# Next chunk's transposes moved from TensorE to the DMA queue, with q/k and output products re-placed, in a fused attention and feed-forward kernel

## The chip, the cores and the metric

The kernel runs on one core of one Trainium2 chip. The metric is the device time of one execution in microseconds. Thirteen runs of the kernel before have a median of 184.62 us, from 183.6 to 185.64.

## The reference

`x` has 2048 positions of 448 features. It is layer-normalised once, and two branches read the result. `_A_ref` is a dilated local attention with 16 heads of 28 features: each position looks at itself and at seven earlier ones, two apart. `_B_ref` is a feed-forward block with 1792 hidden features. The branches are multiplied and added to the input.

```python
xn = _layernorm(x, axis=-1)
# _A_ref(xn): H = 16; Dh = 28; W, dil = 8, 2
qkv = (xn @ wqkv)...                       # 448 -> 3*448
idx = pos[:, None] - off[None, :]          # off = 0, 2, ..., 14
logits = einsum("bhsd,bhswd->bhsw", q, k[idx]) * Dh ** -0.5   # masked where idx < 0
o = einsum("bhsw,bhswd->bhsd", softmax(logits), v[idx])
s = o.reshape(B, S, D) @ wo
# _B_ref(xn):
h = gelu(xn @ w1 + b1)                     # 448 -> 1792, tanh form
g = silu(h @ w2 + b2)                      # 1792 -> 448
out = x + s * g
```

## The kernel before

**Tiles and chunks.** The even positions are put first and the odd ones after them, so that the dilation becomes a plain window of eight. The 2048 rows are 16 tiles of 128 and four chunks of four tiles. The feature dimension of 448 is four blocks of up to 128 (`KT`); the last is repeated to fill 128 rows, so that two products with 64 rows can run beside each other (`ffn1_rest`, L233).

**Layer norm.** For a tile, `ln_stats` (VectorE) and `ln_rstd` (ScalarE) give mean and scale, and `ln_apply` (L164) writes the normalised rows to `xnb`, of which there are four. `ln_tr` (L172) turns them with four TensorE transposes into a PSUM tile `pT`, and `ln_put` (L176) copies that to `xnT`, features by positions. All products read `xnT`.

**Attention.** `q_job` and `k_job` make four heads of q or k for one chunk: four matmuls of 512 columns (L188) and a copy from PSUM (L191). `v_job` makes v for one unit (L203, L208). A unit is 121 positions; there are 17. `qk_unit` computes the scores of all heads into two `psA` tiles (L312), `Exp` on ScalarE (L317) and a mask on VectorE (L319). `av_unit` multiplies with v into `psO` (L328) and spreads the denominators (L332); the `norm` that it returns is two ScalarE operations (L335, L336) and one on VectorE (L337), which writes `oT`.

**Feed-forward.** `feed_forward_1(c, ...)` is the first product of chunk c, in seven steps k of two hidden tiles each; `gelu` (L239) reads each from PSUM and writes `hT`. `ffn2_job(t)` is the second product of tile t (L257, 14 matmuls) with the bias added on VectorE (L264); `silu_job` is a tanh on ScalarE (L268) and an operation on VectorE (L269). `wo_job(t)` is the output product (L288), the multiplication with the feed-forward branch and the addition of x (L294, L297), and the store (L298).

**PSUM.** `psA` has two tiles of two banks, shared by scores and feed-forward steps. `psB` has four tiles of one bank for everything else; steps k = 0, 3 and 6 of the first product take two of them each.

**Order.** The instructions of TensorE, ScalarE, VectorE and GpSimd run in the order in which the program is written. The loads and stores are on the SP queue; the 16 loads of `wo` (L134) are the last of the loads in it. Chunk 0 is prepared with TensorE transposes and ScalarE copies. Then for c = 0, 1, 2: `feed_forward_1(c)`, with the four tiles' transposes of chunk c+1 in steps 0 and 2 (two tiles after each), silu of chunk c-1 in the same steps, and four q/k jobs of chunk c+1 in step 4; then the phase change with two more q/k jobs; then five attention units, beside which stand the second products of chunk c, the last q/k jobs and the v jobs of chunk c+1. `feed_forward_1(3)`, two units and the remaining output products end the program. The Gelu and the Exp operations need different ScalarE tables, so each `feed_forward_1` has a table load at either end (L351, L377). In chunks 2 and 3 the list `wos` gives output products to the steps from k = 2 on.

At the start `busy(8)` gives TensorE matmuls on zeros. A memset of eight pad columns of `wraw` (L125) stands in VectorE's order after the loads were issued.

Of the kernel before, what the change touches and what calls it, by code (L numbers as in the profile page):

```python
# [8 lines left out]
F32 = mybir.dt.float32  # L9
# [13 lines left out]
QB = 121  # L23
QW = 122
NB = 17
LEAD = 8
LQ = LEAD + S + 24
SCALE = 1.0 / math.sqrt(DH)
EPS = 1e-5
NG = 12  # L30
# [3 lines left out]
def kernel(  # L34
# [19 lines left out]
    def dram_rows(par, t0, n):  # L54
        cls, r = divmod(t0 * P, S // 2)
        return par[cls, r:r + n * P, :].rearrange("(t p) d -> p t d", p=P)
# [36 lines left out]
        return x_sb[t // 4][:, t % 4, :]  # L93


    nc.vector.memset(wz[:].bitcast(U32), 0)
    nc.vector.memset(eps_t[:], EPS)
    for t in range(4):
        (nc.sync, nc.scalar)[t % 2].dma_start(x_sb[0][:, t, :], dram_rows(x_par, t, 1)[:, 0, :])
    for dst, c0, c1 in ((wv, 2 * D, 3 * D), (wraw, 0, 2 * D)):  # L100
        nc.sync.dma_start(dst[:, 0:3, 0:c1 - c0], A_wqkv[0:384, c0:c1].rearrange("(k p) f -> p k f", p=P))
        nc.sync.dma_start(dst[:64, 3, 0:c1 - c0], A_wqkv[384:448, c0:c1])
    nc.sync.dma_start(b1t[:], B_b1.rearrange("(m f) -> f m", f=P))
    for c0, c1 in ((0, F // 2), (F // 2, F)):
        nc.sync.dma_start(w1[:, 0:3, c0:c1], B_w1[0:384, c0:c1].rearrange("(k p) f -> p k f", p=P))
        for r in (0, 64):
            nc.sync.dma_start(w1[r:r + 64, 3, c0:c1], B_w1[384:448, c0:c1])
        if c0 == 0:
            nc.sync.dma_start(x_sb[1][:, :, :], dram_rows(x_par, 4, 4))
    nc.sync.dma_start(w2[:, :, :], B_w2.rearrange("(m p) c -> p m c", p=P))  # L110
    nc.sync.dma_start(b2bc[:], B_b2.rearrange("(o d) -> o d", o=1).to_broadcast((P, D)))
    nc.sync.dma_start(x_sb[2][:, :, :], dram_rows(x_par, 8, 4))
# [9 lines left out]
    nc.gpsimd.memset(vw[:, :, :, 0:1], 1.0)  # L122
    nc.gpsimd.memset(vw[:, :, :, DH + 1:32], 0.0)
    nc.vector.memset(wv[64:128, 3, :].bitcast(U32), 0)
    nc.vector.memset(wraw[:, :, 2 * D:2 * D + 8].bitcast(U32), 0)  # L125
    nc.vector.memset(wraw[64:128, 3, 0:2 * D].bitcast(U32), 0)
    nc.vector.memset(wo[:, :, :].bitcast(U32), 0)
    for tl in (qT, kT):
# [25 lines left out]
    def ln_stats(t):  # L154
        st = work.tile([P, 6], F32, name="st", tag="st", bufs=4)
        nc.vector.bn_stats(out=st[:], in_=xt(t))
        nc.vector.bn_aggr(out=mv[:, t, :], in_=st[:])
# [11 lines left out]
    def ln_tr(t):  # L169
        pT = psB.tile([P, KT, P], BF16, name="pT", tag="B")  # L170
        for kt in range(KT):
            nc.tensor.transpose(pT[:, kt, :], xnb[t % 4][:, kt * P:(kt + 1) * P], ident[:])  # L172
        return pT

    def ln_put(t, pT, copy):
        copy(xnT[:, :, LEAD + t * P:LEAD + (t + 1) * P], pT[:, :, :])  # L176


    def qk_weights(which, kt):
# [13 lines left out]
    def q_job(c, g):  # L193
        qk_job(c, g, 0, nc.vector.tensor_copy)

    def k_job(c, g, copy=None):
        qk_job(c, g, 1, copy or nc.scalar.copy)
# [14 lines left out]


    def ffn1_tiles(k):
        if k % 3 == 0:
            return [psB.tile([P, CH], F32, name="ps_h", tag="B") for _ in range(2)]
        ps = psA.tile([P, 2, CH], F32, name="ps_h", tag="A")
        return [ps[:, i, :] for i in range(2)]
# [47 lines left out]
    def silu_job(t):  # L266
        th = work.tile([P, D], BF16, name="th", tag="th", bufs=2)
        nc.scalar.activation(th[:], y_sb[:, t % 4, 0:D], ACT.Tanh, scale=0.5)  # L268
        nc.vector.scalar_tensor_tensor(out=g_sb[t % NG][:], in0=th[:], scalar=1.0, in1=y_sb[:, t % 4, 0:D],  # L269
                                       op0=ALU.add, op1=ALU.mult)  # L270
# [72 lines left out]
    def busy(n):  # L343

        ps = psB.tile([P, CH], F32, name="ps_w", tag="B")
        for _ in range(n):
            nc.tensor.matmul(ps[:, :], wz[:, 0:P], wz[:, :], start=True, stop=True)

    def feed_forward_1(c, ps, wos):

        nc.scalar.preload_act_table_set(SET_GELU)  # L351
        nx = 4 * (c + 1)
        gelu(0, ps)
        for k in range(0, MT // 2, 2):
            if k:
                ps = ffn1_even(c, k)
                gelu(k, ps)
            if k + 1 < MT // 2:
                ps = ffn1_odd(c, k + 1)
                gelu(k + 1, ps)  # L360
            if c + 1 < NC and k < 4:
                for j in (k, k + 1):
                    ln_put(nx + j, ln_tr(nx + j), nc.vector.tensor_copy)
            if c and k < 4:
                silu_job(4 * (c - 1) + k)
                silu_job(4 * (c - 1) + k + 1)
            if c + 1 < NC and k == 4:
                for g in range(2):
                    q_job(c + 1, g)
                    k_job(c + 1, g, nc.vector.tensor_copy)  # L370
            if c + 2 < NC and 2 <= k < 6:
                ln_stats(nx + 4 + k - 2)
                ln_stats(nx + 4 + k - 1)
            for _ in range(2):
                if k >= 2 and wos:
                    wo_job(wos.pop(0))
        nc.scalar.preload_act_table_set(SET_EXP)  # L377
        if c + 2 < NC:
            ln_rstd(nx + 4, 4)


    with tc.manual_schedule(engines={ENG.PE, ENG.Activation, ENG.DVE, ENG.Pool}):
        nc.scalar.preload_act_table_set(SET_EXP)
        busy(8)
        ln_stats(0)
        ln_rstd(0, 1)
        ln_stats(1)
        ln_rstd(1, 1)
        ln_apply(0)
        pT = [ln_tr(0)]  # L390
        ln_put(0, pT[0], nc.scalar.copy)
        ln_stats(2)
        ln_rstd(2, 1)
        ln_apply(1)
        pT.append(ln_tr(1))
        v0 = v_mm(0)
        ln_put(1, pT[1], nc.scalar.copy)
        ln_stats(3)
        ln_rstd(3, 1)
        v_put(0, v0)  # L400
        ln_apply(2)
        pT.append(ln_tr(2))
        v1 = v_mm(1)
        ln_put(2, pT[2], nc.scalar.copy)
        v_put(1, v1)
        ln_apply(3)
        pT.append(ln_tr(3))
        v2 = v_mm(2)
        ln_put(3, pT[3], nc.scalar.copy)
        v_put(2, v2)  # L410
        v_job(3)
        for which in range(2):
            for kt in range(KT):
                qk_weights(which, kt)
        y_sb = work.tile([P, 4, D + 4], F32, name="y", tag="stage", bufs=1)
        late_constants()
        for g in range(4):
            q_job(0, g)
            if g == 3:
                ln_stats(7)  # L420
                ln_rstd(4, 4)
            else:
                ln_stats(4 + g)
            k_job(0, g)
        ps = ffn1_even(0, 0)
        for t in range(4, 8):
            ln_apply(t)

        units = iter(range(NB))
        for c in range(3):  # L430
            feed_forward_1(c, ps, [0, 1, 2] if c == 2 else [])
            n = c + 1
            beside = [lambda: q_job(n, 3), lambda: k_job(n, 3), lambda: v_job(4 * n), lambda: v_job(4 * n + 1)]
            if c == 2:
                beside[1] = lambda: (k_job(3, 3), v_job(12))
                beside[2] = lambda: v_job(13)
                beside[3] = lambda: v_job(14)
            q_job(n, 2)
            k_job(n, 2)
            norm = lambda: None  # L440
            for i in range(4):
                b = next(units)
                E = qk_unit(b)
                norm()
                ffn2_job(4 * c + i)
                beside[i]()
                if n + 1 < NC:
                    ln_apply(4 * n + 4 + i)
                norm = av_unit(b, E)
            b = next(units)  # L450
            va, vb = 4 * n + 2 + (c == 2), 4 * n + 3 + (c == 2)
            E = qk_unit(b, lambda: v_job(va))
            v_job(vb)
            norm()
            ps = ffn1_even(n, 0)
            norm = av_unit(b, E)
            norm()
        feed_forward_1(3, ps, [3, 4, 5, 6, 7])
        wo_job(8)
        E = qk_unit(15)  # L460
        ffn2_job(12)
        s9 = wo_mm(9)
        norm = av_unit(15, E)
        wo_put(9, s9)
        E = qk_unit(16)
        norm()
        g12 = silu_exp_job(12)
        ffn2_job(13)
        g12()
        s10 = wo_mm(10)  # L470
        norm = av_unit(16, E)
        norm()
        wo_put(10, s10)
        nc.scalar.preload_act_table_set(SET_GELU)
        s11 = wo_mm(11)
        y14 = ffn2_job(14, False)
        wo_put(11, s11)
        s12 = wo_mm(12)
        ffn2_put(14, y14)
        wo_put(12, s12)  # L480
        silu_job(13)
        silu_job(14)
        s13 = wo_mm(13)
        wo_put(13, s13)
        y15 = ffn2_job(15, False)
        s14 = wo_mm(14)
        s15 = wo_mm(15)
        ffn2_put(15, y15)
        wo_put(14, s14)
        silu_job(15)  # L490
        wo_put(15, s15)

# [1 line left out]
_INS = ['A_x', 'A_wqkv', 'A_wo', 'B_x', 'B_w1', 'B_b1', 'B_w2', 'B_b2']  # L494
# [26 lines left out]
```

## Time and profile before

| what | before |
|---|---|
| median of 13 runs | 184.62 us (183.6 to 185.64) |
| the profiled execution's own time | 184.14 us |
| its span in the profile | 182.5 us |
| TensorE busy | 165.6 us (91%) |
| ScalarE busy | 125.4 us (69%) |
| VectorE busy | 118.0 us (65%) |
| first attention unit's scores start | 39.66 us |
| last store issued | 179.65 us, by the end of its VectorE operation |

The span is the time from the first to the last event of the profiled execution; the device time of that execution lies 1.6 us above it, and the median of all runs 0.5 us above that. Busy times are unions of the intervals in which an engine has an instruction; a busy TensorE can still be waiting inside a pipelined group, so pitches between matmuls (from the start of one group to the start of the next) say more than their mean durations. In a line of the timeline the first number is the start and the second the length in microseconds, and the bracket at its end is the idle time of the engine before it and what ended that.

### The profile page before, as it was taken

How to read it: one execution, taken by the hardware profiler on the slowest of the kernel's cores; microseconds unless marked ns; L12 is line 12 of the kernel's file. 1: busy time of each engine (PE TensorE's matmuls, PEld its weight loads, DVE VectorE, ACT ScalarE, POOL GpSimd, SP SyncE). 2: the span in 40 equal slices, each digit the busy share in tenths (PEclk: the TensorE clock that was granted, in tenths of full speed). 3: DMA queues.
4: the chain of work that ended last, by engine and by line, in shares of the span. 5: the costliest groups of instructions: out<-in, count | busy, mean ns of one | idle time of the engine just before them, and what ended most of it. 6: DMA issues, size and time to landing. Idle time of an engine off the chain costs nothing.

```text
span 182.5 us, 3260 instructions
## 1 busy us (share of the span) xinstructions
PE 165.6 (91%) x1308; PEld 76.6 (42%) x1324; DVE 118.0 (65%) x266; ACT 125.4 (69%) x197; POOL 4.5 (2%) x16
## 2 busy tenths in 40 slices
PE   7669999999999789999999679999999999999870
PEld 2234444444555334444544334444555343355430
DVE  6563864456888436938886546728676425977793
ACT  3624297466888699396879796186788699767620
POOL 6002000000000000000000000000000000000000
PEclk9999999999999999999999999999999999999998
DMA  5999952000000000000000000000000000210021
GB/s 151 223 267 322 363 170 44 0 0 5 0 4 0 0 0 4 0 0 0 4 0 4 2 0 25 25 29 0 4 0 0 4 2 0 101 54 25 25 75 50
DMA packets 10990, 9.03 MB, mean 50 GB/s; under 512 B 2592, under 2 KB 10976, under 8 KB 10976
## 3 DMA queue, kind: packets, MB, share of 16 engines
q1 hardware_dynamic: 10688, 8.61, 16.1%
q10 hardware_dynamic: 288, 0.23, 0.4%
q8 instruction: 10, 0.16, 0.4%
q14 instruction: 4, 0.03, 0.1%
HBM read 7.00 MB, written 1.84 MB: 48 GB/s over the span
## 4 chain that ended last, share of the span: by engine, by line
PE 59%; ACT 24%; DVE 8%; DMA 4%; issue 2%; SPq 1%; DVEq 0%
PE ps_y L257 18%; PE ps_qk L188 12%; PE ps_h L224 11%; ACT E L317 6%; ACT hT L239 5%; PE ps_v L203 5%; DMA wraw<-in_A_wqkv_dram 4%; PE ps_s L288 4%; PE S L312 3%; ACT den L336 3%; PE ps_h L233 3%; ACT den L335 2%; PE psO L328 2%; DVE sg L294 2%; DVE g L269 2%
## 5 line engine op out<-in xcount | busy, mean ns | idle before, releaser
L239 ACT ACTIVATE hT<-ps_h,b1f 128x512 bf16<-128x512 f32 x56 | 34.4, 700 | 15.7 <-PE ps_h L233 14.9
L257 PE MATMUL ps_y<-w,hT 128*128 128x448 bf16 x224 | 45.1, 353 | 0.0
L224 PE MATMUL ps_h<-xnT,w 128*128 128x512 bf16 x160 | 40.4, 380 | 0.6
L317 ACT ACTIVATE E<-S 128x976 bf16<-128x976 f32 x34 | 32.0, 986 | 7.3 <-PE S L312 6.3
L188 PE MATMUL ps_qk<-xnT,wqk 128*128 128x512 bf16 x120 | 29.2, 379 | 0.4
L257 PEld LDWEIGHTS <-hT 128*128 128x128 bf16 x224 | 20.8, 98 | 19.3
L319 DVE TENSOR_TENSOR E<-E,mk_gen 128x976 bf16<-128x976 bf16 x30 | 19.8, 665 | 10.8 <-ACT E L317 10.8
L224 PEld LDWEIGHTS <-w 128*128 128x128 bf16 x168 | 15.2, 98 | 20.1 <-issue 4.8
L337 DVE TENSOR_TENSOR oT<-psO,den 128x484 bf16<-128x484 f32 (+1 forms) x17 | 11.2, 661 | 12.4 <-ACT den L336 12.4
L188 PEld LDWEIGHTS <-wqk 128*128 128x128 bf16 x128 | 12.3, 98 | 14.7 <-issue 0.7
L269 DVE SCALAR_TENSOR_TENSOR g<-th,y 128x448 bf16<-128x448 bf16 x15 | 8.7, 621 | 13.7 <-ACT th L268 13.7
L191 DVE CAST qT<-ps_qk 128x512 bf16<-128x512 f32 x16 | 11.0, 686 | 9.4 <-PE ps_qk L188 9.4
L203 PE MATMUL ps_v<-wv,xnT 128*128 128x448 bf16 x68 | 17.0, 387 | 0.0
L288 PE MATMUL ps_s<-wo,oT 128*128 128x448 bf16 x64 | 13.9, 353 | 1.5 <-DVE xnT L176 1.0
L335 ACT ACTIVATE den<-den 128x484 f32<-128x484 f32 (+1 forms) x17 | 10.4, 611 | 5.3 <-DVE den L332 5.3
L208 ACT CAST vw<-ps_v 128x448 bf16<-128x448 f32 x17 | 9.1, 537 | 5.5 <-PE ps_v L203 5.5
L172 PE MATMUL pT<-ident,xnb 128*128 128x128 bf16 x64 | 6.5, 242 | 6.8 <-DVE oT L337 3.4
L332 DVE STREAM_SHUFFLE den<-psO 128x484 f32<-128x484 f32 (+1 forms) x17 | 11.8, 695 | 0.0
L268 ACT ACTIVATE th<-y 128x448 bf16<-128x448 f32 x15 | 8.2, 600 | 4.3 <-DVE y L264 4.3
L336 ACT ACTIVATE den<-den 128x484 f32<-128x484 f32 (+1 forms) x17 | 10.3, 605 | 0.5
L233 PE MATMUL ps_h<-xnT,w 64*128 64x512 bf16 x56 | 9.9, 384 | 0.5 <-ACT hT L239 0.2
L294 DVE SCALAR_TENSOR_TENSOR sg<-ps_s,g 128x448 bf16<-128x448 f32 x16 | 9.9, 616 | 0.2
(60 smaller groups left out, 132.2 us busy)
## 6 DMA issues: line engine op xcount, KB each, us to landing
out_dram<-o_t SPq DMA_DIRECT2D x16, 112.0 KB
w<-in_B_w_dram SPq DMA_DIRECT2D x1, 1568.0 KB
w<-in_B_w_dram SPq DMA_DIRECT2D x2, 672.0 KB
x<-in_A_x_dram SPq DMA_DIRECT2D x3, 448.0 KB
wraw<-in_A_wqkv_dram SPq DMA_DIRECT2D x1, 672.0 KB
w<-in_B_w_dram SPq DMA_DIRECT2D x4, 112.0 KB
wo<-in_A_wo_dram SPq DMA_DIRECT2D x16, 24.5 KB
wv<-in_A_wqkv_dram SPq DMA_DIRECT2D x1, 336.0 KB
```

The source lines that it names most:

```text
L188: nc.tensor.matmul(ps[:, :], wqk[:, kt, 16 * which + 4 * g:16 * which + 4 * g + 4, :], xnT[:, kt, LEAD + c * CH:LEAD + (c + 1) * CH], star ...
L203: nc.tensor.matmul(ps[:, :], xnT[:, kt, o:o + P], wv[:, kt, :], start=(kt == 0), stop=(kt == KT - 1))
L224: nc.tensor.matmul(ps[i][:, :], w1[:, kt, m * P:(m + 1) * P], xnT[:, kt, LEAD + c * CH:LEAD + (c + 1) * CH], start=(first and kt == 0), st ...
L233: nc.tensor.matmul(ps[i][:, :], w1[r, 3, m * P:(m + 1) * P], xnT[r, 3, LEAD + c * CH:LEAD + (c + 1) * CH], start=first, stop=not first)
L239: nc.scalar.activation(hT[:, m, :], ps[i][:, :], ACT.Gelu_apprx_tanh, bias=b1f[:, m:m + 1])
L257: nc.tensor.matmul(ps[:, :], hT[:, m, tt * P:(tt + 1) * P], w2[:, m, :], start=(m == 0), stop=(m == MT - 1))
L288: nc.tensor.matmul(ps[:, :], oT[:, g, t * P:(t + 1) * P], wo[:, g, :], start=(g == 0), stop=(g == 3))
L294: nc.vector.scalar_tensor_tensor(out=sg[:], in0=ps[:, :], scalar=0.5, in1=g_sb[t % NG][:], op0=ALU.mult, op1=ALU.mult)
L317: nc.scalar.activation(ev, Sp[p2][:, :, :, 0:QW], ACT.Exp, scale=SCALE)
L319: nc.vector.tensor_tensor(out=ev, in0=ev, in1=mkb, op=ALU.mult)
L335: nc.scalar.activation(den[:, :, 0:n], den[:, :, 0:n], ACT.Ln)
L336: nc.scalar.activation(den[:, :, 0:n], den[:, :, 0:n], ACT.Exp, scale=-1.0)
```

## The change

- **Transposes of chunks 1 to 3.** After each `ln_apply(t)` for t from 4 on, a new `ln_dma(t)` issues one DMA transpose on the SP queue, from `xnb` to `xnT`. `ln_tr` and `ln_put` remain for chunk 0 alone. The pad ahead of the positions (`LEAD`) goes from 8 to 16 columns.
- **q/k products.** The four jobs in step 4 of `feed_forward_1` go to the phase change, where six stand in a row (g = 0, 1, 2); the k copies there are all on VectorE. The jobs of g = 3 stay beside the units.
- **Silu and statistics.** Silu of the chunk before moves from steps 0 and 2 to steps 2 and 4, the statistics of the chunk after the next from steps 2 and 4 to 0 and 2.
- **Output products.** 0 and 1 go into `feed_forward_1(1)`, 2 and 3 into `feed_forward_1(2)`, 4 to 7 beside units 14 and 15, 8 to 10 into `feed_forward_1(3)`, 11 to 15 to the end. The output products inside `feed_forward_1` start at k = 4 instead of 2.
- **Units.** The chunks hold 5, 5, 6 and 1 units, where they held 5, 5, 5 and 2.
- **PSUM.** Step k = 6 takes a `psA` tile instead of two of `psB`.
- **Start.** The memset of the pad of `wraw` is the first VectorE instruction; the load of x for chunk 1 goes ahead of those of `b1` and `w1`; `busy(9)` replaces `busy(8)`, and `busy(2)` follows the first tile's transposes.
- **End.** The last tile's second product is computed in two halves of 224 columns after output product 15, and tanh, multiplications, addition and store follow for each half. The sixteenth output is stored as two DMAs.

```diff
-LEAD = 8
-LQ = LEAD + S + 24
+LEAD = 16
+LQ = LEAD + S + 16
...
+    nc.vector.memset(wraw[:, :, 2 * D:2 * D + 8].bitcast(U32), 0)
     nc.vector.memset(wz[:].bitcast(U32), 0)
...
+    nc.sync.dma_start(x_sb[1][:, :, :], dram_rows(x_par, 4, 4))
     nc.sync.dma_start(b1t[:], B_b1.rearrange("(m f) -> f m", f=P))
     for c0, c1 in ((0, F // 2), (F // 2, F)):
...
-        if c0 == 0:
-            nc.sync.dma_start(x_sb[1][:, :, :], dram_rows(x_par, 4, 4))
...
-    nc.vector.memset(wraw[:, :, 2 * D:2 * D + 8].bitcast(U32), 0)
...
+    def ln_dma(t):
+        nc.sync.dma_start_transpose(xnT[:, :, LEAD + t * P:LEAD + (t + 1) * P], xnb[t % 4][:, :])
...
     def ffn1_tiles(k):
-        if k % 3 == 0:
+        if k in (0, 3):
...
-            if c + 1 < NC and k < 4:
-                for j in (k, k + 1):
-                    ln_put(nx + j, ln_tr(nx + j), nc.vector.tensor_copy)
-            if c and k < 4:
-                silu_job(4 * (c - 1) + k)
-                silu_job(4 * (c - 1) + k + 1)
-            if c + 1 < NC and k == 4:
-                for g in range(2):
-                    q_job(c + 1, g)
-                    k_job(c + 1, g, nc.vector.tensor_copy)
-            if c + 2 < NC and 2 <= k < 6:
-                ln_stats(nx + 4 + k - 2)
-                ln_stats(nx + 4 + k - 1)
+            if c + 2 < NC and k < 4:
+                ln_stats(nx + 4 + k)
+                ln_stats(nx + 5 + k)
+            if k in (2, 4):
+                if c:
+                    silu_job(4 * (c - 1) + k - 2)
+                    silu_job(4 * (c - 1) + k - 1)
             for _ in range(2):
-                if k >= 2 and wos:
+                if k >= 4 and wos:
                     wo_job(wos.pop(0))
...
         for t in range(4, 8):
             ln_apply(t)
+            ln_dma(t)
...
+        beside = {
+            0: [(ffn2_job, 0, q3, 1), (ffn2_job, 1, k3, 1), (ffn2_job, 2, v_job, 4), (ffn2_job, 3, v_job, 5)],
+            1: [(ffn2_job, 4, q3, 2), (ffn2_job, 5, k3, 2), (ffn2_job, 6, v_job, 8), (ffn2_job, 7, v_job, 9)],
+            2: [(ffn2_job, 8, q3, 3), (ffn2_job, 9, k3, 3, v_job, 12), (ffn2_job, 10, v_job, 13),
+                (ffn2_job, 11, v_job, 14), (wo_job, 4, wo_job, 5, v_job, 15, wo_job, 6)],
+        }
         for c in range(3):
-            feed_forward_1(c, ps, [0, 1, 2] if c == 2 else [])
+            feed_forward_1(c, ps, [[], [0, 1], [2, 3]][c])
...
-            q_job(n, 2)
-            k_job(n, 2)
+            for g in range(3):
+                q_job(n, g)
+                k_job(n, g, nc.vector.tensor_copy)
...
+            else:
+                E = qk_unit(b, lambda: v_job(16))
+                norm()
+                wo_job(7)
...
-        feed_forward_1(3, ps, [3, 4, 5, 6, 7])
-        wo_job(8)
-        E = qk_unit(15)
+        feed_forward_1(3, ps, [8, 9, 10])
         ffn2_job(12)
...
+        s15 = wo_mm(15)
...
+        for cs in (slice(0, hw), slice(hw, D)):
+            yp = psB.tile([P, hw], F32, name="ps_y15", tag="B")
+            for m in range(MT):
+                nc.tensor.matmul(yp[:, :], hT[:, m, 3 * P:4 * P], w2[:, m, cs],
+                                 start=(m == 0), stop=(m == MT - 1))
+            y = y_sb[:, 3, cs]
+            nc.vector.tensor_tensor(out=y, in0=yp[:, :], in1=b2bc[:, cs], op=ALU.add)
+            nc.scalar.activation(th[:, cs], y, ACT.Tanh, scale=0.5)
...
+            nc.vector.tensor_tensor(out=o_t[:, cs], in0=xt(15)[:, cs], in1=g[:, cs], op=ALU.add)
+            nc.sync.dma_start(dram_rows(out_par, 15, 1)[:, 0, cs], o_t[:, cs])
```

More of the change, by code (lines that the diff above doesn't have):

```diff
@@ L173, in ln_tr, with ln_put @@
         return pT
-    def ln_put(t, pT, copy):
-        copy(xnT[:, :, LEAD + t * P:LEAD + (t + 1) * P], pT[:, :, :])
+    def ln_put(t, pT):
+        nc.scalar.copy(xnT[:, :, LEAD + t * P:LEAD + (t + 1) * P], pT[:, :, :])
+    def ln_dma(t):
+        nc.sync.dma_start_transpose(xnT[:, :, LEAD + t * P:LEAD + (t + 1) * P], xnb[t % 4][:, :])
     def qk_weights(which, kt):
@@ L383 @@
         nc.scalar.preload_act_table_set(SET_EXP)
-        busy(8)
+        busy(9)
         ln_stats(0)
@@ L390 @@
         pT = [ln_tr(0)]
-        ln_put(0, pT[0], nc.scalar.copy)
+        busy(2)
+        ln_put(0, pT[0])
         ln_stats(2)
@@ L396 @@
         v0 = v_mm(0)
-        ln_put(1, pT[1], nc.scalar.copy)
+        ln_put(1, pT[1])
         ln_stats(3)
@@ L403 @@
         v1 = v_mm(1)
-        ln_put(2, pT[2], nc.scalar.copy)
+        ln_put(2, pT[2])
         v_put(1, v1)
@@ L408 @@
         v2 = v_mm(2)
-        ln_put(3, pT[3], nc.scalar.copy)
+        ln_put(3, pT[3])
         v_put(2, v2)
@@ L427, with q3, k3 @@
             ln_apply(t)
+            ln_dma(t)
         units = iter(range(NB))
+        def q3(n):
+            q_job(n, 3)
+        def k3(n):
+            k_job(n, 3)
+        beside = {
[4 more added lines that the diff above has]
+        }
         for c in range(3):
-            feed_forward_1(c, ps, [0, 1, 2] if c == 2 else [])
+            feed_forward_1(c, ps, [[], [0, 1], [2, 3]][c])
             n = c + 1
[L433 to L437, printed above, removed]
-            q_job(n, 2)
-            k_job(n, 2)
+            for g in range(3):
+                q_job(n, g)
+                k_job(n, g, nc.vector.tensor_copy)
             norm = lambda: None
-            for i in range(4):
+            for i, jobs in enumerate(beside[c]):
                 b = next(units)
@@ L444 @@
                 norm()
-                ffn2_job(4 * c + i)
-                beside[i]()
-                if n + 1 < NC:
+                for f, t in zip(jobs[::2], jobs[1::2]):
+                    f(t)
+                if n + 1 < NC and i < 4:
                     ln_apply(4 * n + 4 + i)
+                    ln_dma(4 * n + 4 + i)
                 norm = av_unit(b, E)
             b = next(units)
[L451 to L454, printed above, removed]
+            if c < 2:
+                E = qk_unit(b, lambda: v_job(4 * n + 2))
+                v_job(4 * n + 3)
+                norm()
+            else:
+                E = qk_unit(b, lambda: v_job(16))
+                norm()
+                wo_job(7)
             ps = ffn1_even(n, 0)
@@ L457 @@
             norm()
-        feed_forward_1(3, ps, [3, 4, 5, 6, 7])
-        wo_job(8)
-        E = qk_unit(15)
+        feed_forward_1(3, ps, [8, 9, 10])
         ffn2_job(12)
-        s9 = wo_mm(9)
-        norm = av_unit(15, E)
-        wo_put(9, s9)
         E = qk_unit(16)
-        norm()
         g12 = silu_exp_job(12)
@@ L469 @@
         g12()
-        s10 = wo_mm(10)
+        s11 = wo_mm(11)
         norm = av_unit(16, E)
+        wo_put(11, s11)
         norm()
-        wo_put(10, s10)
         nc.scalar.preload_act_table_set(SET_GELU)
-        s11 = wo_mm(11)
         y14 = ffn2_job(14, False)
-        wo_put(11, s11)
+        silu_job(13)
         s12 = wo_mm(12)
@@ L480 @@
         wo_put(12, s12)
-        silu_job(13)
         silu_job(14)
@@ L484 @@
         wo_put(13, s13)
-        y15 = ffn2_job(15, False)
         s14 = wo_mm(14)
+        wo_put(14, s14)
+        hw = D // 2
         s15 = wo_mm(15)
[L488 to L491, printed above, removed]
+        g = g_sb[15 % NG]
+        th = work.tile([P, D], BF16, name="th", tag="th", bufs=2)
+        o_t = work.tile([P, D], BF16, name="o_t", tag="o_t", bufs=3)
+        for cs in (slice(0, hw), slice(hw, D)):
[6 more added lines that the diff above has]
+            nc.scalar.activation(th[:, cs], y, ACT.Tanh, scale=0.5)
+            t0 = work.tile([P, hw], F32, name="t0", tag="t0", bufs=2)
+            nc.vector.scalar_tensor_tensor(out=t0[:], in0=s15[:, cs], scalar=0.5, in1=y,
+                                           op0=ALU.mult, op1=ALU.mult)
+            nc.vector.scalar_tensor_tensor(out=g[:, cs], in0=th[:, cs], scalar=1.0, in1=t0[:],
+                                           op0=ALU.add, op1=ALU.mult)
+            nc.vector.tensor_tensor(out=o_t[:, cs], in0=xt(15)[:, cs], in1=g[:, cs], op=ALU.add)
+            nc.sync.dma_start(dram_rows(out_par, 15, 1)[:, 0, cs], o_t[:, cs])
 _INS = ['A_x', 'A_wqkv', 'A_wo', 'B_x', 'B_w1', 'B_b1', 'B_w2', 'B_b2']
```

## The prediction

> **What bounds the kernel now.** I read the page's busy times and its chain first, then the waits, then the timeline of the stages that the change touches. The page:
>
> ```profile
> PE 165.6 (91%) x1308; PEld 76.6 (42%) x1324; DVE 118.0 (65%) x266; ACT 125.4 (69%) x197; POOL 4.5 (2%) x16
> ...
> PE 59%; ACT 24%; DVE 8%; DMA 4%; issue 2%; SPq 1%; DVEq 0%
> ```
>
> TensorE (PE) carries most of the chain; the rest is ScalarE (ACT) at the stage borders, VectorE (DVE) at the end and one load at the start. The timeline shows the places (start, length, engine, line, operation, idle time before it):
>
> ```profile
> 10.46 0.07 DVE L125 MEMSET wraw<- 128x16 uint32 x1 [3.09 <-DMA wraw<-in_A_wqkv_dram]
> ...
> 19.70 10.12 SPq L134 DMA_DIRECT2D wo<-in_A_wo_dram  x16
> ...
> 37.93 1.26 ACT L239 ACTIVATE hT<-ps_h,b1f 128x512 bf16<-128x512 f32 x2 [3.80 <-PE ps_h L233]
> ...
> 64.59 0.40 PE L172 MATMUL pT<-ident,xnb 128*128 128x128 bf16 x4 [1.73 <-DVE oT L337]
> ...
> 71.73 3.62 PE L188 MATMUL ps_qk<-xnT,wqk 128*128 128x512 bf16 x16
> ...
> 178.61 0.62 DVE L294 SCALAR_TENSOR_TENSOR sg<-ps_s,g 128x448 bf16<-128x448 f32 x1
> 179.26 0.39 DVE L297 TENSOR_TENSOR o_t<-x,sg 128x448 bf16<-128x448 bf16 x1
> ```
>
> To be seen: a pad memset that waits 3.09 us for a load and holds VectorE; the SP queue busy with `wo` loads until 29.8; ScalarE idle while TensorE makes q/k products in step 4; a transpose that waits for a `psB` tile held by the last unit; a VectorE end. The waits say how large the third is over the kernel (us, times, longest):
>
> ```profile
> ACT hT L239 <- PE ps_h L233: 14.9, 6, 4.6
> ```
>
> **What the Trainium skill says.** "DMA: Bandwidth & Descriptors", section "DMA Transpose (X-bar)", wants a destination aligned to 32 bytes: the new `LEAD` of 16 two-byte columns is that, 8 was not. No DMA transpose is in this trace. "VectorE: DVE Perf Modes", section "The three transpose paths", prices a 128x128 block at 1309 ns by DMA and 390 on TensorE; here TensorE takes 242 ns for one alone (the row of L172) and 0.45 us for eight in a stream. "TensorE: Matmul & The Clock Gate", Part 1, says that TensorE falls to half clock after about 3.4 us of idling. The trace agrees as far as it goes: the matmuls of `busy` are 0.43 us apart (3.0 to 3.4 us), those of `q_job` at 15 to 22 us 0.22.
>
> **Start.** With the memset (0.07) ahead, `ln_apply(2)` starts at 7.4 (end of the statistics) instead of 10.5. The q products then wait for the `wraw` load (10.38), eight copies of 0.21 us pitch on VectorE (1.7) and the transposes and v products; I take 12.7 for their start instead of 15.16: a gain of 2.5 (1.5 to 3.1). The three extra `busy` matmuls cost at most 0.3 of it. x of chunk 1 goes ahead of `w1`, whose first half SP issues by 10.1 here and which is first needed at about 19.6: nothing under that cover, 1.3 without it (448 KB at the 363 GB/s of the busiest slice).
>
> **First product of chunk 0.** 32 q/k matmuls at 0.216 us are 6.9: `feed_forward_1(0)` starts at 19.6. A step is six matmuls of 0.216 and two paired ones, 1.62 us; seven are 11.3. Sixteen transposes (0.9 in the chain) and 16 q/k matmuls (3.45) are gone from it, so TensorE stands before the six q/k jobs at **30.9**. ScalarE started gelu at about 22.7 and ends it at 32.0, hidden. Six jobs are 24 x 0.216 = 5.2.
>
> **The transposes of chunk 1.** Each q/k matmul reads all four tiles of its chunk, so it waits for the fourth DMA transpose. These stand on SP behind the 16 `wo` loads, which end at 29.8 whatever TensorE does; `ln_apply(4..7)` is done by 23. I take an issue pitch like that of the `wo` loads (10.12/16 = 0.63) and 1.3 from the last issue to landing (SP's last wait for `out_dram`, 1.3): 29.8 + 4 x 0.63 + 1.3 = **33.6**. Bounds: from below 30.9, no wait; from above, the page's 1309 ns once for an instruction, 29.8 + 4 x 1.31 + 1.3 = 36.3, or once for each 128x128 block, 29.8 + 16 x 1.31 + 1.3 = 52. Scores of unit 0 start at 33.6 + 5.2 = 38.8 (39.66 before). Then come 0.35 scores, 2.75 second product, 0.87 q job: `psO` at 42.8. Before it was 44.03, because ScalarE was late there. **-1.3.** Behind the waiting product stand the other jobs, the scores and with them ScalarE's `Exp`; nothing else can fill TensorE. Chunks 2 and 3 have one transpose for every unit of 4.2 us and need them 15 us later: hidden unless one takes over 4.2 us. `ln_apply(8)`, at 45, must wait until `xnb` has been read, with the masks behind it on VectorE: covered by the same product. Stores stand behind transposes on SP only in chunk 1 and later, where a transpose of 0.6 or 1.3 delays them by that, with no reader.
>
> **Chunk 1** (times of the profile). Gelu can start at 65.14 as before. 14 gelus at 0.605 and four tanh at 0.53 make 10.6: ScalarE, not TensorE, now sets the product and ends it at 75.8 (78.3 before). The transposes' 1.73 us wait is gone, but step 4 waits about 1.5 us for its `psA` tile until gelu 1 is read. TensorE comes to the q/k jobs at 74.0. Their VectorE copies stand behind the two silu operations (until 75.25) and two output products' 0.96 each: 77.15. With four `psB` tiles the jobs stretch from 5.2 to 5.5; scores at 79.5, then as above `psO` at 83.5 against 83.10. **+0.4**, with two output products (2 x 0.76 of TensorE) done early. The three k copies that go from ScalarE (0.58) to VectorE (0.69) are inside this.
>
> **Chunk 2.** Before, it had the same shape plus three output products and ended 39.07 + 2.96 us after chunk 1; `psO` at 125.13. Now it repeats chunk 1: 83.5 + 39.07 = 122.6. **-2.5.**
>
> **Unit 14 to the end.** From unit 14's scores (138.82) to gelu before: 8.2 us. Now unit 15 (0.66) and four output products (3.04 on TensorE) come between, and VectorE decides: four times 0.96 beside masks of 0.66, spreads of 0.70 and `oT` of 0.66, so the mask of unit 15 comes 2 us late and its `psO` waits for a `psB` tile. I get gelu 14.1 us after unit 14's scores, **+5.95**. The first product is bound by ScalarE as above and has three output products instead of six, `wo_job(8)` counted; TensorE reaches `ffn2_job(12)` 9.6 us after the gelu start. Then unit 16, four second products (11.0) and five output products (3.8) are 15.5. VectorE is the last again: from tanh 13 at 173.0 its operations in order (silu 0.6, bias 0.6, products 0.96) run until 179.65 in the first half and 181.1 in the second, and a store takes 2.85 (182.5 - 179.65): 183.95 against 182.5. **+1.45.** The halves save about 1.1 there, already in it (operations of 0.35 instead of 0.6).
>
> **Sum.** -1.3 + 0.4 - 2.5 + 1.45 = -1.95: span 180.5, 1.6 us around it as in the profiled execution (184.14 for 182.5), and the median 0.5 above that: **182.6**.
>
> **Rivals.**
> *The transposes come later than TensorE by so much that the start's gain and more is lost (slower).* SP is the bound. The gain of the start and of the transposes is worth nothing once the fourth lands after 30.9: from there each microsecond counts whole. The sum is zero at 33.6 + 1.95 = **35.6**. With the page's price per instruction, 36.3, it is +0.7; TensorE then idles 5.4 us, which by the page on the clock gate means half clock for the next 3.4 us, an estimated 1.7 more: +2.4, in all **187.0**. For it: SP's `wo` loads do end at 29.8, and a transpose has more to do than a load. Against: nothing in this trace; a plain 128-row load takes 0.4 to 0.6 us on SP. With the price per block +16: 201.
> *The transposes are hidden.* If SP takes them ahead of some of the `wo` loads, whose first use is now at 71, nothing waits: scores at 36.1, `psO` at 40.1, -3.9 and in all -4.5: **180.1**. Against it: the loads stand first in the program, and on the SP row they follow each other without a gap that xnb's readiness could fill.
> *The moves do nothing.* ScalarE already has 125 us, and my gain in chunk 2 rests on a first product that ScalarE alone sets. If copies and tiles hold TensorE as long as before, chunk 2 gains only the third output product's 0.8, the sum is -1.3 + 0.4 - 0.8 + 1.45 = -0.25, and the whole is **184.4**, no change.
>
> **How the numbers follow.** Landing near 33.6 (32 to 35): 0.36, 182.6. Hidden: 0.17, 180.1. Late by 36 or more: 0.34, of which 0.05 by the block price. Moves without effect: 0.13. A difference of 0.3% is 0.55 us, about what a measurement of this kernel can tell from no change. Faster: most of the first two, a little of the last, 0.51. Same: a part of each border, 0.10. Slower: 0.39. Both signs hold much; the first case's own range is 180.8 to 184.2. The range for all leaves out the block price and the lowest hidden values: 178.6 to 188.2.
>
> **What would show it.** In the timeline after: `ln_apply(2)` before 8 us; the first q product near 12.7; L172 with 16 matmuls, L176 without VectorE; SP rows of four transposes after the last `wo`, and their length, which decides all; the idle time before the first q product of chunk 1, 2.7 if I am right, 0 if hidden, over 5 if SP is the bound, and then matmuls 0.43 apart; ScalarE without idle time before L239 in chunks 1 to 3, and the q copies there behind L294; unit 0's `psO` at 42.8. I am wrong if chunk 1's first product still ends with ScalarE waiting for TensorE, or if the tail from unit 14 is no longer than before.

## The result, and the profile after

The changed kernel takes **187.29 us** (median of 11 runs, 186.12 to 188.22); the kernel before, beside it, 184.52. The ratio is 1.0139, with a 95% interval of 1.0114 to 1.0164: **slower by 1.4%**. The forecast was 182.6 and faster. The rival with the late transposes gave 187.0.

The profiled execution of the changed kernel has a span of 186.3 us and a time of 188.01, 0.7 above its median, while that of before (184.14) lay 0.4 below the median of its own runs. So the spans differ by 3.8 us and the medians by 2.8; the steps below are measured in spans.

From the page after: busy time by engine, the TensorE clock granted in 40 slices of the span (tenths of full speed), and the chain by engine.

```profile
PE 163.8 (88%) x1279; PEld 75.0 (40%) x1293; DVE 116.6 (63%) x261; ACT 123.8 (66%) x195; POOL 4.5 (2%) x16
...
PEclk9999999559999999999999999999999999999999
...
PE 53%; ACT 19%; SPq 11%; DMA 6%; DVE 6%; issue 3%; DVEq 0%; ACTq 0%
```

TensorE has 1.8 us less to do, and its share of the chain fell from 59 to 53%. The SP queue has risen from 1 to 11%: a queue has entered the chain. Two slices, 33 to 42 us, run at half clock. The timeline of the changed kernel shows why (start, length, engine, line, operation, idle time before it):

```profile
10.99 7.07 PE L190 MATMUL ps_qk<-xnT,wqk 128*128 128x512 bf16 x31
...
28.99 0.39 PE L235 MATMUL ps_h<-xnT,w 64*128 64x512 bf16 x2
...
30.77 5.22 SPq L178 DMA_TRANSPOSE xnT<-xnb  x4
...
37.35 8.03 PE L190 MATMUL ps_qk<-xnT,wqk 128*128 128x512 bf16 x23 [7.97 <-DMA xnT<-xnb]
...
45.31 0.39 PE L314 MATMUL S<-qT,kT 28*128 28x122 bf16 x16
...
49.26 0.40 PE L330 MATMUL psO<-E,vw 128*32 128x122 bf16 x16
```

The same two places in the kernel before:

```profile
15.16 7.07 PE L188 MATMUL ps_qk<-xnT,wqk 128*128 128x512 bf16 x31
...
44.03 0.39 PE L328 MATMUL psO<-E,vw 128*32 128x122 bf16 x14 [0.19 <-DVE E L319]
```

The q products of chunk 0 start at 10.99 instead of 15.16, and the first product of chunk 0 is through at 29.4. The four transposes of chunk 1 are taken up at 30.77 and occupy SP for 5.22 us, 1.305 each. When their data can be read, at 37.35, TensorE has been idle for 7.97 us, and the matmuls that follow are slow. In stretches of the changed kernel (length, then busy time and count of PE, PEld, DVE, ACT, POOL, then the granted clock, the DMA share and GB/s):

```profile
29.40:37.30 7.90, 0.00 (x0) 0.00 (x0) 0.00 (x0) 3.05 (x5) 0.00 (x0) 0.70 0.47 84
37.30:42.80 5.50, 5.45 (x13) 1.90 (x14) 1.52 (x3) 0.00 (x0) 0.00 (x0) 0.50 0.00 0
42.80:45.30 2.50, 2.45 (x11) 0.98 (x10) 1.94 (x3) 0.00 (x0) 0.00 (x0) 0.99 0.00 0
```

Thirteen matmuls in 5.5 us at clock 0.50, then eleven in 2.5 at 0.99: the six jobs take 7.96 us instead of the 5.2 of 24 matmuls at 0.216.

In the waits of the changed kernel (us in total, times, longest), ScalarE's 14.9 us before gelu have become 0.8; TensorE now waits for gelu:

```profile
PE ps_qk L190 <- DMA xnT<-xnb: 8.0, 1, 8.0
...
PE ps_h L226 <- ACT hT L241: 3.7, 3, 1.2
...
ACT hT L241 <- PE ps_h L235: 0.8, 2, 0.4
```

Cut at the same instructions in both profiles, the difference of 3.8 us is made up like this (`psO` is a unit's product with v; before, two of the sixteen matmuls of unit 0's start at 43.61 and the others, which the mask holds up, at 44.03, which is taken here and in the prediction):

| stretch | before | after | difference | forecast |
|---|---|---|---|---|
| start to `psO` of unit 0 | 44.03 | 49.26 | +5.23 | -1.3 |
| from there to `psO` of unit 10 (chunks 1 and 2) | 81.10 | 78.56 | -2.54 | -2.1 as summed, -2.5 as worked out |
| to the scores of unit 14 | 13.69 | 13.69 | 0 | 0 |
| from there to the end | 43.7 | 44.8 | +1.1 | +1.45 |

Only the first row is far off, by 6.5 us.

### The profile page after: what moved, and what is told of

Its sections match the earlier page's. It is cut to its first block, busy times and chain, and to the rows that moved or that the text cites. A ratio compares the mean times of both kernels' runs of the same rounds, so it can differ in the third digit from the quotient of the medians.

```text
span 186.3 us, 3220 instructions
## 1 busy us (share of the span) xinstructions
PE 163.8 (88%) x1279; PEld 75.0 (40%) x1293; DVE 116.6 (63%) x261; ACT 123.8 (66%) x195; POOL 4.5 (2%) x16
## 4 chain that ended last, share of the span: by engine, by line
PE 53%; ACT 19%; SPq 11%; DMA 6%; DVE 6%; issue 3%; DVEq 0%; ACTq 0%
PE ps_y L259 19%; PE ps_qk L190 13%; PE ps_h L226 7%; ACT E L319 5%; DMA x<-in_A_x_dram 5%; ACT hT L241 4%; PE ps_s L290 4%; PE S L314 3%; PE ps_v L205 3%; SPq L107 3%; ACT den L338 3%; ACT den L337 2%; PE psO L330 2%; ACT L353 2%; SPq L178 2%
## 5 line engine op out<-in xcount | busy, mean ns | idle before, releaser
L226 PE MATMUL ps_h<-xnT,w 128*128 128x512 bf16 x161 | 39.4, 380 | 4.2 <-ACT hT L241 3.7
L259 PE MATMUL ps_y<-w,hT 128*128 128x448 bf16 x210 | 42.3, 353 | 0.0
L190 PE MATMUL ps_qk<-xnT,wqk 128*128 128x512 bf16 x121 | 31.6, 406 | 8.3 <-DMA xnT<-xnb 8.0
L241 ACT ACTIVATE hT<-ps_h,b1f 128x512 bf16<-128x512 f32 x56 | 33.9, 707 | 1.6 <-PE ps_h L235 0.8
L259 PEld LDWEIGHTS <-hT 128*128 128x128 bf16 x210 | 19.4, 98 | 18.0
L190 PEld LDWEIGHTS <-wqk 128*128 128x128 bf16 x128 | 12.9, 103 | 24.8 <-issue 12.3
L205 PE MATMUL ps_v<-wv,xnT 128*128 128x448 bf16 x68 | 15.4, 353 | 0.1
L290 PE MATMUL ps_s<-wo,oT 128*128 128x448 bf16 x64 | 13.8, 353 | 1.4 <-ACT vw L210 1.1
L155 DVE BATCH_NORM_STATS2 st<-x 128x6 f32<-128x448 bf16 x16 | 9.7, 609 | 4.6 <-DMA x<-in_A_x_dram 4.6
L334 DVE STREAM_SHUFFLE den<-psO 128x484 f32<-128x484 f32 (+1 forms) x17 | 11.8, 695 | 0.0
L266 DVE TENSOR_TENSOR y<-ps_y,b2bc 128x448 f32<-128x448 f32 x15 | 9.3, 617 | 0.8 <-PE ps_y L259 0.8
L296 DVE SCALAR_TENSOR_TENSOR sg<-ps_s,g 128x448 bf16<-128x448 f32 x15 | 9.2, 615 | 0.0
```

The costliest lines, as they stand in the source:

```text
L190: nc.tensor.matmul(ps[:, :], wqk[:, kt, 16 * which + 4 * g:16 * which + 4 * g + 4, :], xnT[:, kt, LEAD + c * CH:LEAD + (c + 1) * CH], star ...
L205: nc.tensor.matmul(ps[:, :], xnT[:, kt, o:o + P], wv[:, kt, :], start=(kt == 0), stop=(kt == KT - 1))
L226: nc.tensor.matmul(ps[i][:, :], w1[:, kt, m * P:(m + 1) * P], xnT[:, kt, LEAD + c * CH:LEAD + (c + 1) * CH], start=(first and kt == 0), st ...
L241: nc.scalar.activation(hT[:, m, :], ps[i][:, :], ACT.Gelu_apprx_tanh, bias=b1f[:, m:m + 1])
L259: nc.tensor.matmul(ps[:, :], hT[:, m, tt * P:(tt + 1) * P], w2[:, m, :], start=(m == 0), stop=(m == MT - 1))
L290: nc.tensor.matmul(ps[:, :], oT[:, g, t * P:(t + 1) * P], wo[:, g, :], start=(g == 0), stop=(g == 3))
```

## The experiments

**Theory:** the loss is chunk 1's DMA transposes, late because of their place in the SP queue, with the half clock that the wait brings; the rest of the change gains. **Rivals:** a DMA transpose comes late whatever its place; the six q/k products in a row cost the time; the matmuls are slow because of the transposes' writes and not for the idle time.

### The wo loads after the transposes (e1_wo_later)

```diff
-    for g in range(4):                      # 16 loads of wo, among the first loads
-        for h in range(4):
-            ...
         for t in range(4, 8):
             ln_apply(t)
             ln_dma(t)
+        load_wo()                           # the same 16 loads
```

> The changed kernel with the 16 loads of wo written after the four DMA transposes of chunk 1, nothing else. Theory (the place in the SP queue made the transposes late): they are issued from about 20.5 us on as the normalised tiles come, the first q product of chunk 1 follows its predecessor at 29.4 without a wait and at full clock, unit 0's psO stands at about 38.6 instead of 49.3, and the median falls from 187.3 by 10.7 to about 176.6. Rival (a DMA transpose is slow by itself, or its data stand behind those of the x and w2 loads in the DMA engines): a wait of several us stays before the first q product, and the median is 183 or more.

177.20 us, 0.9587 of before (0.9558 to 0.9615): 10 us less than the changed kernel. Its timeline:

```profile
19.46 1.54 SPq L134 DMA_DIRECT2D wo<-in_A_wo_dram  x2
...
21.11 5.80 SPq L179 DMA_TRANSPOSE xnT<-xnb  x4
...
26.96 6.13 SPq L134 DMA_DIRECT2D wo<-in_A_wo_dram  x14
...
29.23 5.35 PE L191 MATMUL ps_qk<-xnT,wqk 128*128 128x512 bf16 x23
```

Two `wo` loads still come first, though the program writes all sixteen behind the transposes; how they get there is not shown. Then come the four transposes and the other loads. The last transpose leaves SP at 26.9; the q product follows its predecessor at 29.23 without a wait, and 24 matmuls take 5.3 us. `psO` of unit 0 stands at 38.46 (38.6 expected). A transpose among loads in flight is thus not late: the place in the queue decides, and the rival falls.

### Chunk 1 on TensorE (e2_pe_chunk1)

```diff
         for t in range(4, 8):
             ln_apply(t)
-            ln_dma(t)
...
+            if c == 0 and k in (2, 4):
+                for j in (k - 2, k - 1):
+                    pt = ln_tr(nx + j)
+                    nc.vector.tensor_copy(xnT[...], pt[:, :, :])
```

> The changed kernel with the transposes of chunk 1 back on TensorE (steps 2 and 4 of the first product of chunk 0, copies on VectorE); chunks 2 and 3 stay on the DMA queue. Theory (all of the loss lies in chunk 1's wait; the DMA transposes of chunks 2 and 3 are hidden): 16 transposes in two streams of eight cost 0.9 us on TensorE, no wait before the q products, psO of unit 0 at about 39.5, median about 177.5. Rival (the six q/k products in a row at the phase change are what costs, not the wait): psO of unit 0 after 44 and a median above 183.

178.14 us, 0.9639 (0.961 to 0.9668). With the same six jobs in a row and no wait ahead of them:

```profile
30.14 5.35 PE L190 MATMUL ps_qk<-xnT,wqk 128*128 128x512 bf16 x23
35.43 0.40 PE L314 MATMUL S<-qT,kT 28*128 28x122 bf16 x16
```

The 24 matmuls take 5.3 us again, so the row of six jobs is not what costs. Against e1 the transposes on TensorE move the scores of unit 0 from 34.52 to 35.43: 0.91 us for 16, the 0.9 that the prediction read from the chain.

### TensorE kept busy while it waits (e3_warm)

```diff
+            if c == 0:
+                busy(34)
             for g in range(3):
                 q_job(n, g)
```

> The changed kernel with 34 matmuls on zeros (34 x 0.216 = 7.3 us) before the q products of chunk 1, so that TensorE does not idle while it waits for the transposes. Theory (the 8 us of idle time halved the clock): the wait ends at the same 37.35, the 24 q/k matmuls take 5.2 us instead of 7.96, and the median falls by 2.8 to 184.5. Rival (the matmuls are slow because they read xnT right after, or while, the DMA engines write it): they stay at 0.43 us apart and the median stays at 187.3.

184.75 us, 1.0021 of before (0.9995 to 1.0048), 2.5 below the changed kernel. The transposes still hold the jobs up: SP takes them up at 30.22, and the first job starts at 36.80. But the clock stays:

```profile
29.20 7.51 PE L349 MATMUL ps_w<-wz 128*128 128x512 bf16 x33
36.80 5.34 PE L190 MATMUL ps_qk<-xnT,wqk 128*128 128x512 bf16 x24
```

The 24 matmuls take 5.3 us though the same transposes have just written what they read. So the half clock came from the idle time, and its price was 7.96 - 5.27 = 2.7 us.

### The memset alone (e4_memset)

```diff
+    nc.vector.memset(wraw[:, :, 2 * D:2 * D + 8].bitcast(U32), 0)
     nc.vector.memset(wz[:].bitcast(U32), 0)
...
-    nc.vector.memset(wraw[:, :, 2 * D:2 * D + 8].bitcast(U32), 0)
```

> The kernel before with the memset of the pad of wraw as the first VectorE instruction, nothing else. Theory: VectorE's wait of 3.09 us goes, chunk 0's first product starts about 3 us earlier than 21.9 and, since TensorE sets the order from there on, the median falls by 2.5 to 3.5, to 181 to 182. Rival (later stages wait for loads or ScalarE and give it back): the first product starts earlier, but the median stays within 1 us of before.

In the kernel before, this one line gives 181.02 us, 0.9788 (0.9747 to 0.9829). The q products start at 12.35 and the scores of unit 0 at 36.85 instead of 39.66; the 2.8 us stay to the end of the span (179.7 instead of 182.5). No later stage gives it back.

### Each transpose in four (e5_split)

```diff
-        nc.sync.dma_start_transpose(xnT[:, :, ...], xnb[t % 4][:, :])
+        for kt in range(KT):
+            nc.sync.dma_start_transpose(xnT[:, kt, ...], xnb[t % 4][:, kt * P:(kt + 1) * P])
```

> The changed kernel (wo loads ahead of the transposes) with each 128x512 DMA transpose written as four of 128x128. In the changed kernel one takes 1.305 us on SP. Theory (the price is one per instruction): 16 instructions in chunk 1 take 16 x 1.305 = 20.9 us from about 30.8, the first q product of chunk 1 starts near 53 instead of 37.4, and the time is about 203. Rival (the price is one per 128x128 block or per byte): 0.33 us each, the same 37.4 and about 187.

One run, 200.9 us (about 203 expected). The matmuls of the first q job, each of which reads one of the four blocks, start as the blocks of the last tile land:

```profile
48.15 0.58 PE L191 MATMUL ps_qk<-xnT,wqk 128*128 128x512 bf16 x1 [18.68 <-DMA xnT<-xnb]
49.42 0.59 PE L191 MATMUL ps_qk<-xnT,wqk 128*128 128x512 bf16 x1 [0.69 <-DMA xnT<-xnb]
50.69 0.58 PE L191 MATMUL ps_qk<-xnT,wqk 128*128 128x512 bf16 x1 [0.68 <-DMA xnT<-xnb]
52.06 6.17 PE L191 MATMUL ps_qk<-xnT,wqk 128*128 128x512 bf16 x21 [0.78 <-DMA xnT<-xnb]
```

They are 1.27 to 1.37 us apart. An instruction with a quarter of the data costs as much as one with the whole: for these two sizes the price is one per instruction.

### The end and the output products

Five edits of e1 ask where the +1.1 from unit 14 to the end comes from. In e6 the last tile is whole, in e7 units and products lie at the end as before, with the halves kept; in e8 and e10 products move from beside units 14 and 15 into the first products. e11 is e10 with unit 15 at the end. The diffs are excerpts; lines between those shown are left out.

```diff
# e6_whole_tail
-        for cs in (slice(0, hw), slice(hw, D)):
-            ...
+        ffn2_job(15)
+        silu_job(15)
+        wo_put(15, s15)
# e7_units_5552
-                (ffn2_job, 11, v_job, 14), (wo_job, 4, wo_job, 5, v_job, 15, wo_job, 6)],
+                (ffn2_job, 11, v_job, 14)],
...
-        feed_forward_1(3, ps, [8, 9, 10])
+        feed_forward_1(3, ps, [4, 5, 6, 7, 8])
+        E = qk_unit(15)
# e8_wo67
-                ... (wo_job, 4, wo_job, 5, v_job, 15, wo_job, 6)],
+                ... (wo_job, 4, wo_job, 5, v_job, 15)],
-                wo_job(7)
-                if k >= 4 and wos:
+                if k >= (2 if c == 3 else 4) and wos:
-        feed_forward_1(3, ps, [8, 9, 10])
+        feed_forward_1(3, ps, [6, 7, 8, 9, 10])
# e10_wo_early
-                ... (wo_job, 4, wo_job, 5, v_job, 15, wo_job, 6)],
+                ... (v_job, 15)],
-                wo_job(7)
-                if k >= 4 and wos:
+                if k >= 2 and wos:
-            feed_forward_1(c, ps, [[], [0, 1], [2, 3]][c])
+            feed_forward_1(c, ps, [[], [0, 1, 2, 3], [4, 5, 6, 7]][c])
# e11_wo_early_5552: e10 with
-                ... (v_job, 15)],
         feed_forward_1(3, ps, [8, 9, 10])
+        E = qk_unit(15)
         ffn2_job(12)
+        norm = av_unit(15, E)
```

e6: 

> The kernel with the wo loads after the transposes (177.2, 0.9587 of before), with the last tile's second product, tanh, multiplications, addition and store whole instead of in two halves of 224 columns. Theory (VectorE is the last engine in the end, and its work is the same either way): the end moves by 0.3 to 0.5 us, median 177.5 to 177.7. Rival (the halves save the 1.1 us that the prediction gave them): 178.3.

e7: 

> The kernel with the wo loads after the transposes (0.9587 of before), with units 15 and 16 and output products 4 to 15 at the end placed as in the kernel before (5, 5, 5, 2 units; products 4 to 8 in the first product of chunk 3 from step 2 on), the halves of the last tile kept. Theory (unit 15 and four output products beside unit 14 overload VectorE, +1.15 us from unit 14 to the end although the halves are in): the stretch from unit 14's scores to the end falls from 44.8 to about 43.2, median 175.6. Rival (the new place is what fills TensorE while ScalarE makes gelu): it rises to 45.5 or more, median 178 or more.

e8: 

> The kernel with the wo loads after the transposes (0.9587 of before), with output products 6 and 7 moved from beside units 14 and 15 into step 2 of the first product of chunk 3, where TensorE waits 1.23 us for a psA tile. Theory (VectorE's two products of 0.96 hold back the masks of unit 15, and step 4's wait covers the TensorE part): gelu of chunk 3 starts 1.5 to 2 us earlier, the end 1 to 1.5 us, median about 176. Rival (the VectorE work is only moved, and comes back at the end): 177.2 or more.

e10: 

> The kernel with the wo loads after the transposes (0.9587 of before), with output products 0 to 3 in the first product of chunk 1, 4 to 7 in that of chunk 2, 8 to 10 in that of chunk 3, all from step 2 on, and none beside units 14 and 15. Theory (the products are free where ScalarE sets the stage and cost where VectorE does): chunks 1 and 2 take 0.3 to 0.8 us longer each, the stretch from unit 14's scores to gelu falls from 13.8 to about 9.5, median about 174.5. Rival (the products fill VectorE in front of the q/k copies and hold up the phase change by more): 176 or more.

e11: 

> The kernel of the run before, with unit 15 back at the end (5, 5, 5, 2 units). Theory (once the output products are gone from there, unit 15 costs the same in either place): within 0.5 us of the run before. Rival (a unit at the end gives TensorE work while ScalarE and VectorE finish): faster by 0.7 us or more.

| kernel | median us | ratio to the before measured beside it (95%) | unit 14's scores to the table load ahead of gelu | unit 14's scores to the end |
|---|---|---|---|---|
| before | 184.52 | | 6.90 | 43.7 |
| e1 | 177.20 | 0.9587 (0.9558 to 0.9615) | 12.50 | 44.8 |
| e6 | 177.41 | 0.9641 (0.9613 to 0.9669) | 12.49 | 45.0 |
| e7 | 175.52 | 0.9534 (0.9504 to 0.9564) | 6.90 | 43.1 |
| e8 | 175.52 | 0.9543 (0.9512 to 0.9573) | 10.69 | 43.1 |
| e10 | 173.97 | 0.9432 (0.94 to 0.9463) | 10.53 | 41.7 |
| e11 | 174.89 | 0.9477 (0.9447 to 0.9508) | 6.90 | 42.2 |

The runs of before beside e1 and those beside e6 to e8 have medians 0.5 us apart, so the stretches of the profiles say more here than medians and ratios. The halves are worth 0.2 us in the stretch on which they act, which may be nothing: the 1.1 of the prediction is refuted. The old place of unit 15 and the products gives 1.7 us back in the stretch (43.1; about 43.2 expected), and moving two products to step 2 gives as much (e8). In the changed kernel VectorE shows what they did there:

```profile
146.50 0.62 DVE L296 SCALAR_TENSOR_TENSOR sg<-ps_s,g 128x448 bf16<-128x448 f32 x1
147.46 0.62 DVE L296 SCALAR_TENSOR_TENSOR sg<-ps_s,g 128x448 bf16<-128x448 f32 x1
...
149.02 1.23 DVE L321 TENSOR_TENSOR E<-E,mk_gen 128x976 bf16<-128x976 bf16 x2
...
151.19 0.40 PE L330 MATMUL psO<-E,vw 128*32 128x122 bf16 x16 [0.97 <-DVE oT L339]
```

Three products, 0.96 each, stand ahead of the masks of unit 15, whose scores start at 146.58; the last two are shown. Its `psO` then waits for `oT` of the unit before, which frees a `psB` tile.

In e10 eight products lie in the first products of chunks 1 and 2, where four did. The distance from `psO` of unit 0 to that of unit 5, and from there to unit 10, is 39.40 and 39.39 us, against 39.29 each in e1: two products more per chunk, 1.5 us of TensorE, cost 0.1 (0.3 to 0.8 expected). They stand in step 2, ahead of the place where TensorE waits 1.25 us for gelu in e1. e10 is the fastest kernel of this study, 5.7% below before. The stretch to the table load falls only to 10.53 (9.5 expected up to gelu, 11.8 measured). Part of that can be the clock. In the profiled execution of e10 one slice lies below full clock, and in it ten matmuls take longer than elsewhere:

```profile
PEclk9999999999999999999999999999999699999999
...
134.78 1.64 PE L206 MATMUL ps_v<-wv,xnT 128*128 128x448 bf16 x4
136.21 2.48 PE L227 MATMUL ps_h<-xnT,w 128*128 128x512 bf16 x6
```

The same ten in e8:

```profile
135.71 0.93 PE L206 MATMUL ps_v<-wv,xnT 128*128 128x448 bf16 x4
136.48 1.46 PE L227 MATMUL ps_h<-xnT,w 128*128 128x512 bf16 x6
```

From 135 to 138 us the granted clock was 0.50, and the ten matmuls took 1.7 us more. So how much of the stretch unit 15 itself costs there stays open. e11 doesn't settle where that unit belongs either: its stretch to the end is 0.5 longer and its median 0.9 higher, against both expectations, but the intervals of the ratios overlap.

### No DMA transpose at all (e9_all_pe)

```diff
-            if c == 0 and k in (2, 4):          # e2
+            if c + 1 < NC and k in (2, 4):
...
                     ln_apply(4 * n + 4 + i)
-                    ln_dma(4 * n + 4 + i)
```

> The changed kernel with the transposes of all chunks on TensorE (steps 2 and 4 of the first product, copies on VectorE), no DMA transpose at all. Theory (apart from chunk 1's wait, the DMA transposes bring no more than the TensorE time they free): against the kernel with chunk 1 alone on TensorE (0.9639 of before) chunks 2 and 3 lose 0.9 us each at most, less where step 4's wait of 1.2 us covers them: 178.5 to 180. Rival (the gain of chunk 2 rests on the DMA transposes): 182 or more.

179.16 us, 0.9704 (0.9668 to 0.9741), as expected. From `psO` of unit 0 to that of unit 5, and to that of unit 10, it takes 39.73 us each, against 39.29 in e2. So the DMA transposes of chunks 2 and 3 are worth 0.44 us a chunk, half of the TensorE time that they free, and of chunk 2's gain over before (42.03 us there) the other 2.3 come from the rest of the change: two output products in the first product instead of three, and the new places of q/k products, silu and tiles. No run takes these apart.

## Why the prediction was wrong

- **The step that failed is "The transposes of chunk 1".** It took a pitch of 0.63 us from the `wo` loads for an operation that the trace didn't show. The measured pitch is 1.305, which makes 2.7 us more for four. The loads ahead of them held SP for 11.04 us instead of 10.12, so that SP was free at 30.77 instead of 29.8; why they took longer is not shown. The landing term was right (37.35 - 35.99 = 1.36 against 1.3). The sum gives 30.77 + 4 x 1.305 + 1.36 = 37.35 instead of 33.6: **3.75 us**.
- **The clock** was counted in the rival alone, since the forecast's idle time was 2.7 us. With 7.97 it came, and cost 2.76 us where the rival estimated 1.7. 3.75 + 2.76 is the whole error of 6.5 us. e3 takes the second part away alone, e1 takes away both.
- "The three transpose paths" of the Trainium skill ("VectorE: DVE Perf Modes") had the price: 1309 ns for a 128x128 block, 1.27 to 1.37 us here (e5). What it doesn't say, and the runs show, is that 128x512 in one instruction takes the same, 1.305. The rival with this price once per instruction was the right reading; the per-block price is refuted. That the rival's 187.0 lies 0.3 from the measured 187.29 is partly luck: its landing (36.3) and its clock were each 1.1 us short, while the later stages came out 0.8 better than counted and the medians lie 1.0 closer together than the spans.
- **The start** gained 4.2 us at the q products, not 2.5. e4 shows 2.8 for the memset. The rest goes with v products at full rate (four in 0.92 us at 7.05, against 1.70 before and also in e4), which fits the added `busy` matmuls; those were not tried alone. All of it was lost in the wait, as the rival said. The first product ended at 29.4, not 30.9.
- **Chunks 1 and 2** were right: +0.21 and -2.75, together -2.54. The working had two slips that cancel. It let chunk 2 repeat the 39.07 of the old chunk 1 and not its own 39.5 for the new one, and so came to -2.5 with chunk 1 already in it; the sum then added +0.4 once more. Measured, chunk 2 does repeat chunk 1: 39.28 each. ScalarE does set these first products, and step 4 does wait for its `psA` tile (1.24 us).
- **Unit 14 to the end** was right in sign and cause: gelu starts 13.8 us after unit 14's scores (14.1 forecast), and the end comes +1.1 for +1.45. Within it, the halves' 1.1 was wrong; VectorE is the last engine there and does the same work in more operations. Without the halves the forecast would have been +2.55, so the rest was counted over 1 us too high, and that the sum comes near is partly luck.
- **The rivals.** "Hidden" needs SP to take the transposes ahead of the loads: e1 is that case, and it gives 177.2, below the 180.1 named, mainly since the start gained more (`psO` of unit 0 at 38.46, not 40.1). "The moves do nothing" allowed chunk 2 a gain of 0.8 us; it gains 2.7 in e2 and 2.3 in e9.

## What to carry to other kernels

Price an operation that a trace doesn't show by the page that names it, not by the nearest row of another operation, and add up the whole queue ahead of it. When a long wait on TensorE is likely, add what the idle time does to its clock (2.7 us here, after 7.97 us). Put products that need VectorE where ScalarE sets the pace, and keep them away from masks that a unit waits for.

## What was not expected of the hardware

After 7.97 us of idle time, TensorE ran at half clock for 5.5 us of continuous matmuls (13 of them). The about 3.4 us of sustained work that the Trainium skill ("TensorE: Matmul & The Clock Gate", Part 1) names for the return to full rate are given there as the least: one whole busy window, of windows that run on whenever the matmuls start. The 1.7 us of the rival were that least price, and 2.7 was paid. The fall of the clock agrees with the page's figure: if the clock was 1 and then 0.50, the mean of 0.70 over the 7.90 us ahead of the matmuls puts its fall about 3.2 us after TensorE went idle (an estimate).

Half clock also came without such a wait. In e10 it was granted from 135 to 138 us, though no idle time of TensorE in the 20 us before was longer than 1.00 us; e8 had one of 1.12 at that place and kept its clock. Why is not shown.

A DMA transpose holds the SP queue for 1.2 to 1.4 us whether it moves 128x128 or 128x512 elements.
